# One engine for both copies of a turned query block, row squares on ACT, and a step's scores at its head: three edits to the attention loop of a fused kernel

## The chip, the core and the metric

The program runs on one core of a Trainium2 chip. The metric is the device time of one execution in microseconds, the median over several runs. Engines are named as the profile names them: PE (matmuls and transposes; PEld is its weight load), DVE (VectorE), ACT (ScalarE), POOL (GpSimd) and SP (which here only issues DMAs). The stages and rows below come from one profiled execution; its time stands beside its span in the table.

## What is computed

Three stages in a row, all in float32:

```python
# 1. attention in a sliding window of 64, q k v: (4, 8, 576, 64)
scores = q @ k.T / 8, masked to 0 <= i - j < 64;  attn = softmax(scores);  x = attn @ v
x = x.transpose(0, 2, 1, 3).reshape(2304, 512)
# 2. mixture of 8 experts, one expert per token
xn = x / (norm(x, axis=-1) + 1e-6)
logits = xn @ normalized(expert_emb).T / tau        # tau = 0.1
expert = argmax(logits);  gate = softmax(logits)[expert]
x = gate * (relu(x @ w1[expert]) @ w2[expert])
# 3. dense layer over all 2304 tokens, 512 -> 2048 -> 512
out = (s * relu(x @ w_in) ** 2 + b) @ w_out
```

## The kernel before

**Stages.** The attention loop takes some 157 us, the end of the routing (which token goes to which expert) some 25 us more, and the experts and the dense layer the rest. This change touches the attention loop alone.

**The attention loop.** The work is cut into 36 steps. A step `n` holds two slots, each a tile of 128 tokens (`t`, 0 to 17) and a pair of heads (`hp`, 0 to 3). PE's order and SP's order are written out by hand (`manual_schedule`); DVE, ACT and POOL are ordered by a planner that runs on its own estimate of a timeline, and each engine then works through its list strictly in order. A step of the loop does this for PE, in this order:

- `prepare(n)`: the next 2 or 3 *pieces*. A piece is one head of `k` or `q` of one unit (a batch and a pair of heads; four pieces to a unit, in the order k0, k1, q0, q1): three transposes into one of three PSUM tiles `tp` (L224), and then two copies of 64x288 to `kT` or `qT` (L229 on ACT, L231 on DVE). The two copies write every other column of the same 64 rows. After a unit's last piece, the loads of the unit after next are issued from SP (`load_qk`, L159), and its `v` loads (L185).
- `flips(n)`: four transposes (L268) of the exponentials `pe` of step `n-2` (from step 31 on, of the step one back), into the one PSUM tile `pt`, which ACT copies to `pT` (L270).
- `run(n, HALF)`: what earlier steps left in a list for this step, kinds `TURN` and `WHOLE`: transposes of finished rows of `x` (L375, copied by ACT at L377), matmuls that count and list tokens (L316), the write of `x` (L677, on SP), the first expert's weight loads (L96, on SP).
- `scores(n)`: 16 matmuls (L241) into one of two halves of `spb`; DVE adds the mask and finds the extremum (L249, four times: `sm`, `mn`); in steps 2 to 30 POOL subtracts it (L252); ACT takes the exponential in `exps` (L259, or four times L262 where POOL did not subtract). In step 4 `router_setup` follows, with its loads on ACT's DMA queue.
- `run(n)`: the list's other kinds, `HALF` (the router's logits, L316) and `BEHIND`.
- `fins(n)`: 16 matmuls (L280) with `v` into the one PSUM tile `po`, for step `n-3`; DVE takes the reciprocal of the sum and scales into `xs` (L283, L284, L289).

**Squares of x.** When the last head pair of a tile is done, the sum of squares of its rows (`ss`) is needed, for the norm in `route_norm` (POOL, L460), then `route_gate` (DVE, L467 and on). For tiles 0 to 10 POOL makes it in `squares`: a product (L394) and nine halving additions (L398) for each pair of tiles. For tiles 11 and 12 DVE makes it in one instruction (L381), for 13 to 15 ACT (L384), for 16 and 17 DVE.

Of the kernel before, what the change touches and what calls it, by code (L numbers as in the profile page):

```python
# [8 lines left out]
F32 = mybir.dt.float32  # L9
# [3 lines left out]
AF = mybir.ActivationFunctionType  # L13
ALU = mybir.AluOpType
# [6 lines left out]
def tile_kernel(ctx, tc, q, k, v, emb, tau, w1, w2, w_in, w_out, s_in, b_in, out, x_dram, y_dram, y0_dram, wi_dram, wo_dram):  # L21
    nc = tc.nc
    B, H, S, D = q.shape
    NT, DM = out.shape
# [11 lines left out]
    TF = 13  # L36
    TL = 16
# [42 lines left out]
    x2p = ctx.enter_context(tc.tile_pool(name="x2p", bufs=1))  # L80
# [59 lines left out]
    lp = al.enter_context(tc.tile_pool(name="lp", bufs=1))  # L140
    la = al.enter_context(tc.tile_pool(name="la", bufs=8))
    aw = ac.enter_context(ExitStack())
    at = aw.enter_context(tc.tile_pool(name="at", bufs=1))
# [70 lines left out]
    xs = {}  # L214

    def prep(b, hp):

        kt, qt = qk.pop((b, hp))
        n = (b * NP + hp) % NB
        for nm, src, dst in (("k", kt, kTs[n]), ("q", qt, qTs[n])):  # L220
            for h in range(2):
                pt = ps3.tile([128, QC, QP], F32, tag="tp", name="tp")
                for c in range(QC):
                    nc.tensor.transpose(pt[:, c], src[:, h, c], ident[:QP, :QP])  # L224
                for par in range(2):
                    o = dst[64 * h:64 * h + 64].rearrange("r (c p e) -> r e c p", c=QC, e=2)[:, par]
                    i = pt[64 * par:64 * par + 64]
                    if par == 0 or (nm, h) in TOACT:
                        nc.scalar.activation(o, i, AF.Copy)  # L229
                    else:  # L230
                        nc.vector.tensor_copy(o, i)  # L231
                yield
# [23 lines left out]
    def exps(sm, mn):  # L256
        pe = at3.tile([128, 4, 128], F32, tag="pe", name="pe")
        if mn is None:
            nc.scalar.activation(pe, sm, AF.Exp, scale=-1.0)  # L259
            return pe  # L260
        for j in range(4):
            nc.scalar.activation(pe[:, j], sm[:, j], AF.Exp, bias=mn[:, j:j + 1], scale=-1.0)  # L262
        return pe
# [51 lines left out]
    def add(out, a, b):  # L315
        nc.tensor.matmul(out, a, b, start=False, stop=True, skip_group_check=True)  # L316
# [7 lines left out]
    ss = rp.tile([128, NTT], F32, name="ss")  # L324
# [43 lines left out]
    def rows_of(t):  # L368
        return xs[t][:, t - FIRST[t]]

    def route_turn(t, lp=None):
        xw = rows_of(t)
        tp = ps3.tile([128, ND, 128], F32, tag="tp", name="tpx")
        for c in range(ND):
            nc.tensor.transpose(tp[:, c], xw[:, c * 128:(c + 1) * 128], ident)  # L375
        xt = (lp or at3).tile([128, ND, 128], F32, tag=f"xt{t}" if lp else "xt", name="xt")
        marks.append(nc.scalar.activation(xt, tp, AF.Copy))  # L377
        if t >= LATE:
            sq = (lp or at).tile([128, DM], F32, tag="sq", name="sq")
            if t < TF or t >= TL:  # L380
                nc.vector.tensor_tensor_reduce(out=sq, in0=xw, in1=xw, scale=1.0, scalar=0.0,  # L381
                                               op0=ALU.mult, op1=ALU.add, accum_out=ss[:, t:t + 1])
            else:
                nc.scalar.activation(sq, xw, AF.Square, accum_out=ss[:, t:t + 1])  # L384
        return xt

    def route_logits(t, xt):
        for c in range(ND):
            for o in range(0, 128, 64):
                add(lg[o:o + 64, t], xt[:, c, o:o + 64], enT[:, c])  # L390

    def squares(t, n):
        sq = x2p.tile([128, 1024], F32, tag="xh", name="sq").rearrange("p (s d) -> p s d", s=2)[:, :n]
        nc.gpsimd.tensor_tensor(sq, xs[t], xs[t], op=ALU.mult)  # L394
        c = DM // 2
        while c >= 1:
            o = ss[:, t:t + n].unsqueeze(2) if c == 1 else sq[:, :, :c]
            nc.gpsimd.tensor_tensor(o, sq[:, :, :c], sq[:, :, c:2 * c], op=ALU.add)  # L398
            c //= 2

    def block(kk, ln, a):

# [19 lines left out]
    def route_count(t0, t1):  # L422
        ts_ = slice(t0, t1)
        add(R[:, ts_].rearrange("p t e -> p (t e)"), tri, oh[:, ts_].rearrange("p t e -> p (t e)"))
        for t in range(t0, t1):
            add(R[:, t + 1:], ones, oh[:, t].unsqueeze(1).to_broadcast([128, NTT - t, E]))
# [28 lines left out]
    def listed(t0, t1, j0, j1, Qv):  # L455
        for t in range(t0, t1):
            add(ls[:, j0:j1], lane[:, t], Qv[:, t - t0])
# [208 lines left out]
    def fin(slots, pT):  # L666
        pv(slots, pT)
        t = slots[0][0]
        if slots[-1][1] < NP - 1:
            return  # L670
        ts_ = sorted({t for t, _ in slots})
        nt = len(ts_)
        if t < LATE:
            squares(t, nt)

        def write():
            nc.sync.dma_start(x_dram[t * 128:(t + nt) * 128].rearrange("(s p) n -> p s n", p=128), xs[t])  # L677

        n = now[0]
        if n < len(steps):  # L680
            later(n + 1, write)
        else:
            write()
        if t == TL:
            return
        xts = {}

        def turned(t):
            xts[t] = route_turn(t)

        for j, k_ in enumerate(ts_):
            m = n + (0 if t >= LATE else j)
            later(m + 1, lambda k_=k_: turned(k_), TURN)
            later(m + 2, lambda k_=k_: route_logits(k_, xts[k_]), HALF)
        if ts_[-1] not in ROUTED:
            return
        (t0, t1), d = ROUTED[ts_[-1]]
        q = []
        later(n + d[0], lambda: route_rank(t0, t1), BEHIND)
        later(n + d[1], lambda: route_count(t0, t1))  # L700
        if t1 == TF:
            later(n + d[1], first_weights)
        later(n + d[2], lambda: route_list(t0, t1))
        later(n + d[3], lambda: q.append(part(t0, t1, 0, 2)))
        later(n + d[4], lambda: listed(t0, t1, 0, 2, q[0]))
        if t1 == TL:
            return
        later(n + d[5], lambda: route_norm(t0, t1))
        later(n + d[6], lambda: route_gate(t0, t1), BEHIND)
        later(n + d[7], lambda: q.append(part(t0, t1, 2, 5)), BEHIND)  # L710
        later(n + d[8], lambda: listed(t0, t1, 2, 5, q[1]))
        if t1 == TF:
            later(n + d[9], first_turn)
            later(n + d[4], first_rows)
# [64 lines left out]
            yield  # L779

    now = [0]
    TOACT = (("k", 0), ("k", 1))

    ROUTED = {3: ((0, 4), (4, 5, 6, 7, 9, 10, 11, 12, 14)),
# [3 lines left out]
    LATE = 11  # L788
# [6 lines left out]
    TURN, WHOLE, HALF, BEHIND = range(4)  # L795

    def later(n, do, kind=WHOLE):
        todo.setdefault(n, []).append((kind, do))

    def run(n, end=9):  # L800

        q = todo.get(n, [])
        for kind in range(end):
            for k_, do in [x for x in q if x[0] == kind]:
                q.remove((k_, do))
                do()
        if not q:
            todo.pop(n, None)
# [13 lines left out]
    need = [4 * (max(u for us in used[:n + 1] for u in us) + 1) for n in range(len(steps))]  # L822
# [32 lines left out]
    def flips(n):  # L855
        while len(pts) < len(steps) and len(pts) + lag(len(pts)) <= n:
            pts.append(flip(pes[len(pts)]))
# [16 lines left out]
    done = [0]  # L874
    pes, pts = [], []

    def prepare(n):
        want = max(need[m] + (AHEAD if m > n else 0) - RATE * (m - n) for m in range(n, len(steps)))
        while done[0] < min(want if n else need[0] + 2, 4 * len(units)) and free(done[0] // 4, n):
            next(pieces)  # L880
            done[0] += 1
        assert done[0] >= need[n]

    with tc.manual_schedule(engines={mybir.EngineType.PE, mybir.EngineType.SP}):
        for n, s in enumerate(steps):
            now[0] = n
            prepare(n)
            t = s[0][0]
            if t not in xs:
                nt = 1 if t == s[1][0] else 2  # L890
                xs[t] = (lp if t == TL else xp).tile([128, nt, DM], F32, tag=f"xs{nt}", name="xs",
                                                            **({} if t == TL else {"bufs": 2 * nt}))
                xs[s[1][0]] = xs[t]
            flips(n)
            run(n, HALF)
            sm, mn = scores(n, s)
            if n == 4:
                router_setup()
            pes.append(exps(sm, mn))
            run(n)  # L900
            fins(n)
            values()
        N = len(steps)
        for n in range(N, N + 2):
            now[0] = n
            flips(n)
            some(n - N)
            fins(n)
            if n in todo:
                run(n)  # L910
# [395 lines left out]
```

## Time and profile before

| | |
|---|---|
| median of 3 runs | 847.34 us (847.22 to 849.98) |
| the profiled execution | 851.04 us, of which its span is 849.2 us |
| PE busy | 790.2 us (93% of the span), mean granted clock 0.961 |
| DVE busy | 516.7 us (61%) |
| ACT busy | 387.1 us (46%) |
| POOL busy | 237.2 us (28%) |

Busy shares are means over stages with different limits: behind the attention and routing PE hardly rests, inside the attention loop it does. The granted clock is PE's: 1.0 is 2.4 GHz, 0.5 is 1.2 GHz, and a mean between them is a share of time at either.

### The profile page before, as it was taken

How to read it: one execution, taken by the hardware profiler on the slowest of the kernel's cores; microseconds unless marked ns; L12 is line 12 of the kernel's file. 1: busy time of each engine (PE TensorE's matmuls, PEld its weight loads, DVE VectorE, ACT ScalarE, POOL GpSimd, SP SyncE). 2: the span in 40 equal slices, each digit the busy share in tenths (PEclk: the TensorE clock that was granted, in tenths of full speed). 3: DMA queues.
4: the chain of work that ended last, by engine and by line, in shares of the span. 5: the costliest groups of instructions: out<-in, count | busy, mean ns of one | idle time of the engine just before them, and what ended most of it. 6: DMA issues, size and time to landing. Idle time of an engine off the chain costs nothing. (4 is left out here: it accounts for less than half of the span.)

```text
span 849.2 us, 16607 instructions
## 1 busy us (share of the span) xinstructions
PE 790.2 (93%) x6350; PEld 724.4 (85%) x6350; DVE 516.7 (61%) x1310; ACT 387.1 (46%) x770; POOL 237.2 (28%) x248
## 2 busy tenths in 40 slices
PE   7887887878999999989899999999999999999996
PEld 5676765778999999979899999999999999999885
DVE  4566586675687787689665555566665444444442
ACT  6686656413435355364364444444445333323331
POOL 3374775241202433434302222122210110101110
PEclk9997897878999999999999999999999999999998
DMA  9865925215749787769265322234323111100000
GB/s 204 191 177 159 218 65 195 88 30 202 244 130 297 238 275 243 271 217 311 99 220 180 100 100 100 79 121 125 124 88 101 61 40 50 50 25 25 26 26 25
DMA packets 100642, 117.16 MB, mean 138 GB/s; under 512 B 38884, under 2 KB 72164, under 8 KB 100560
## 3 DMA queue, kind: packets, MB, share of 16 engines
q1 hardware_dynamic: 91072, 99.11, 38.7%
q0 software_dynamic: 3232, 10.24, 3.5%
q10 hardware_dynamic: 6256, 6.72, 2.4%
q8 instruction: 51, 0.84, 0.4%
q14 instruction: 31, 0.25, 0.1%
HBM read 91.52 MB, written 24.53 MB: 137 GB/s over the span
## 5 line engine op out<-in xcount | busy, mean ns | idle before, releaser
L126 PE MATMUL p<-xl,wh 128*128 128x256 f32 x576 | 162.4, 282 | 0.0
L126 PE MATMUL p<-xh,wh 128*128 128x256 f32 x576 | 162.2, 282 | 0.0
L126 PE MATMUL p<-xh,wl 128*128 128x256 f32 x576 | 161.7, 281 | 0.0
L1213 ACT ACTIVATE r<-p 128x256 f32<-128x256 f32 x144 | 55.2, 384 | 167.9 <-PE p L126 163.6
L1214 DVE SCALAR_TENSOR_TENSOR r<-r,s_bc 128x256 f32<-128x256 f32 x144 | 79.9, 558 | 78.0 <-ACT r L1213 77.6
L1037 POOL TENSOR_TENSOR fl<-fl,fs 128x512 f32<-128x512 f32 x32 | 45.9, 1436 | 251.7 <-DVE fs L1036 219.3
L126 PE MATMUL p<-wh,gh 128*128 128x512 f32 x288 | 113.0, 392 | 0.0
L126 PE MATMUL p<-wl,gh 128*128 128x512 f32 x288 | 113.0, 392 | 0.0
L126 PE MATMUL p<-wh,gl 128*128 128x512 f32 x288 | 113.0, 392 | 0.0
L126 PEld LDWEIGHTS p<-xh,wh 128*128 128x128 f32 x576 | 108.8, 189 | 0.7
L126 PEld LDWEIGHTS p<-xl,wh 128*128 128x128 f32 x576 | 108.6, 189 | 0.8
L126 PEld LDWEIGHTS p<-xh,wl 128*128 128x128 f32 x576 | 109.0, 189 | 0.0
L88 DVE TENSOR_TENSOR wl<-raw,wh 128x1024 fp32r<-128x1024 f32 x72 | 102.8, 1433 | 6.0 <-ACT wh L87 5.7
L87 ACT ACTIVATE wh<-raw 128x1024 fp32r<-128x1024 f32 x80 | 83.4, 1057 | 6.4 <-DMA raw<-wo_dram 2.3
L126 PE MATMUL p<-hh,wh 128*128 128x256 f32 (+5 forms) x256 | 78.7, 307 | 0.0
L126 PE MATMUL p<-hl,wh 128*128 128x256 f32 (+5 forms) x256 | 76.9, 301 | 0.0
L126 PE MATMUL p<-hh,wl 128*128 128x256 f32 (+5 forms) x256 | 76.9, 300 | 0.0
L1220 ACT ACTIVATE gh<-r,b_bc 128x256 fp32r<-128x256 f32 x144 | 72.5, 503 | 7.2 <-DVE r L1214 6.9
L1252 POOL DMA_INDIRECT out_dram<-o,ids x18 | 18.8, 1047 | 203.8 <-DVE o L1251 182.4
L1221 DVE SCALAR_TENSOR_TENSOR gl<-r,b_bc,gh 128x256 fp32r<-128x256 f32 x144 | 71.2, 495 | 3.1 <-ACT gh L1220 3.1
L132 PE MATMUL tp<-xh,wh 128*128 128x256 f32 (+6 forms) x288 | 55.9, 319 | 12.2 <-DVE hl L749 5.5
L126 PEld LDWEIGHTS p<-wh,gl 128*128 128x128 f32 x288 | 54.1, 188 | 12.2
(225 smaller groups left out, 1522.2 us busy)
## 6 DMA issues: line engine op xcount, KB each, us to landing
raw<-in_moe_w_dram SPq DMA_DIRECT2D x64, 512.0 KB, 4.9
raw<-y_dram SPq DMA_DIRECT2D x18, 512.0 KB, 3.8
vb<-in_v_dram SPq DMA_DIRECT2D x64, 128.0 KB, 3.8
fr<-in_moe_w_in_dram SPq DMA_DIRECT2D x16, 512.0 KB, 5.3
fr<-in_moe_w_out_dram SPq DMA_DIRECT2D x16, 512.0 KB, 4.1
k<-in_k_dram SPq DMA_DIRECT2D x32, 144.0 KB, 3.5
q<-in_q_dram SPq DMA_DIRECT2D x32, 144.0 KB, 3.4
x_dram<-xs SPq DMA_DIRECT2D x8, 512.0 KB, 3.1
```

Of the source, the lines that this page charges most:

```text
L87: a = nc.scalar.activation(hi, src, AF.Copy)
L88: return a.ins, le.tensor_tensor(lo, src, hi.bitcast(F32), op=ALU.subtract).ins
L126: nc.tensor.matmul(ps, a[x], b[y], start=first and j == 0, stop=last and j == 2)
L132: nc.tensor.matmul(ps, x, y, start=j == 0, stop=j == len(k) - 1)
L1037: nc.gpsimd.tensor_tensor(lf, lf, sg.bitcast(F32), op=ALU.mult)
L1213: nc.scalar.activation(r, ps, AF.Relu)
L1214: nc.vector.scalar_tensor_tensor(r, r, s_bc, r, op0=ALU.mult, op1=ALU.mult)
L1220: nc.scalar.activation(gh, r, AF.Identity, bias=b_bc)
L1221: nc.vector.scalar_tensor_tensor(gl, r, b_bc, gh.bitcast(F32), op0=ALU.add, op1=ALU.subtract)
L1252: nc.gpsimd.indirect_dma_start(out=out, out_offset=bass.IndirectOffsetOnAxis(ap=ids[:, k:k + 1], axis=0), in_=o, in_offset=None)
```

## The change

Three edits.

1. In `prep`, the copies of piece q0 go both to ACT and those of q1 both to DVE. Before, each of the two pieces had its first copy on ACT and its second on DVE. The number of copies on either engine stays as it is: per unit six on ACT and two on DVE.
2. `squares` is gone; in `route_turn` ACT makes the sum of squares for every tile up to 15 (one `Square` with an accumulator each). That takes the work of tiles 0 to 10 from POOL and that of 11 and 12 from DVE.
3. A step of the loop begins with `scores(n)` and `exps`, unless a piece that they need is still missing; then come `prepare(n)`, `flips(n)` and the whole of `run(n)`. By the loop's own arithmetic no piece is missing in steps 1 to 35.

```diff
@@ prep
-                    if par == 0 or (nm, h) in TOACT:
+                    if (nm, h) in TOACT:
                         nc.scalar.activation(o, i, AF.Copy)
                     else:
                         nc.vector.tensor_copy(o, i)
@@ route_turn
-        if t >= LATE:
-            sq = (lp or at).tile([128, DM], F32, tag="sq", name="sq")
-            if t < TF or t >= TL:
-                nc.vector.tensor_tensor_reduce(out=sq, in0=xw, in1=xw, scale=1.0, scalar=0.0,
-                                               op0=ALU.mult, op1=ALU.add, accum_out=ss[:, t:t + 1])
-            else:
-                nc.scalar.activation(sq, xw, AF.Square, accum_out=ss[:, t:t + 1])
+        sq = (lp or at).tile([128, DM], F32, tag="sq", name="sq")
+        if t >= TL:
+            nc.vector.tensor_tensor_reduce(out=sq, in0=xw, in1=xw, scale=1.0, scalar=0.0,
+                                           op0=ALU.mult, op1=ALU.add, accum_out=ss[:, t:t + 1])
+        else:
+            nc.scalar.activation(sq, xw, AF.Square, accum_out=ss[:, t:t + 1])
@@ squares, and its call in fin
-    def squares(t, n):
-        sq = x2p.tile([128, 1024], F32, tag="xh", name="sq").rearrange("p (s d) -> p s d", s=2)[:, :n]
-        nc.gpsimd.tensor_tensor(sq, xs[t], xs[t], op=ALU.mult)
-        c = DM // 2
-        while c >= 1:
-            o = ss[:, t:t + n].unsqueeze(2) if c == 1 else sq[:, :, :c]
-            nc.gpsimd.tensor_tensor(o, sq[:, :, :c], sq[:, :, c:2 * c], op=ALU.add)
-            c //= 2
...
-        if t < LATE:
-            squares(t, nt)
...
-    TOACT = (("k", 0), ("k", 1))
+    TOACT = (("k", 0), ("k", 1), ("q", 0))
@@ the loop over steps
-            prepare(n)
+            if done[0] < need[n]:
+                prepare(n)
...
-            flips(n)
-            run(n, HALF)
             sm, mn = scores(n, s)
             if n == 4:
                 router_setup()
             pes.append(exps(sm, mn))
+            prepare(n)
+            flips(n)
             run(n)
             fins(n)
```

## Rows read from the trace of the kernel before

**Rows 1.** Stages: length, busy of PE, PEld, DVE, ACT, POOL; granted clock; DMA.

```profile
21.26:42.77 21.51, 17.72 (x263) 13.57 (x262) 12.61 (x74) 14.88 (x32) 7.83 (x11) 0.92 0.84 191
42.77:57.88 15.11, 13.39 (x248) 11.10 (x248) 9.28 (x54) 12.09 (x26) 13.86 (x24) 1.00 0.80 213
76.24:98.94 22.70, 20.10 (x321) 16.70 (x320) 12.47 (x67) 16.72 (x37) 17.43 (x26) 0.88 0.79 193
116.88:130.54 13.66, 10.92 (x195) 9.37 (x194) 11.10 (x51) 6.63 (x13) 10.35 (x14) 0.88 0.21 79
130.54:157.28 26.74, 21.65 (x282) 17.45 (x279) 17.85 (x97) 16.91 (x39) 11.48 (x6) 0.70 0.59 204
175.78:849.20 673.42, 653.61 (x4392) 613.30 (x4391) 399.33 (x727) 277.24 (x539) 141.86 (x105) 0.98 0.41 133
```

**Rows 2.** Waits of PE from 0 to 200 us: total, times, longest.

```profile
PE tp L224 <- DMA k<-in_k_dram: 2.0, 1, 2.0
PE spb L241 <- DVE mn L249: 1.4, 4, 0.5
```

**Rows 3.** Timeline of ACT around 24 us: start, length, idle before and its releaser.

```profile
22.42 0.43 ACT L229 ACTIVATE qT<-tp 64x288 f32<-64x288 f32 x1
...
25.53 0.63 ACT L259 ACTIVATE pe<-sm 128x512 f32<-128x512 f32 x1 [2.21 <-POOL sm L252]
26.19 0.41 ACT L229 ACTIVATE qT<-tp 64x288 f32<-64x288 f32 x1
```

**Rows 4.** Timeline of DVE in the same stretch.

```profile
22.89 0.46 DVE L231 COPY qT<-tp 64x288 f32<-64x288 f32 x1 [1.59 <-ACT qT L229]
23.38 0.29 DVE L249 CUSTOM_DVE_ANT_0 sm<-spb,mask 128x128 f32<-128x128 f32 x1
...
26.63 0.46 DVE L231 COPY qT<-tp 64x288 f32<-64x288 f32 x1 [1.42 <-ACT qT L229]
```

**Rows 5.** Timeline of POOL in the same stretch.

```profile
24.46 1.04 POOL L252 TENSOR_TENSOR sm<-sm,mn 128x512 f32<-128x512 f32 x1 [2.72 <-DVE mn L249]
```

**Rows 6.** Groups by line and shape, 0 to 160 us: busy, mean ns, idle before.

```profile
L259 ACT ACTIVATE pe<-sm 128x512 f32<-128x512 f32 x29 | 18.2, 628 | 16.1 <-POOL sm L252 15.9
...
L231 DVE COPY qT<-tp 64x288 f32<-64x288 f32 x32 | 14.7, 461 | 22.5 <-ACT qT L229 22.1
...
L381 DVE CUSTOM_DVE_ANT_0 sq<-xs 128x512 f32<-128x512 f32 x2 | 2.2, 1076 | 0.1
```

**Rows 7.** Groups of ACT by line and shape, the whole span.

```profile
L384 ACT ACTIVATE sq<-xs 128x512 f32<-128x512 f32 x3 | 1.9, 627 | 0.1
L166 ACT ACT_TABLE_LOAD x1 | 1.3, 1283 | 1.7 <-PEq L1286 1.7
L384 ACT ACTIVATION_READ_ACCUMULATOR sq<-xs 128x1 f32 x3 | 0.6, 192 | 0.0
```

**Rows 8.** Groups of POOL by line, 40 to 130 us.

```profile
L398 POOL TENSOR_TENSOR sq<-sq 128x256 f32<-128x256 f32 (+8 forms) x48 | 22.6, 470 | 2.9
L394 POOL TENSOR_TENSOR sq<-xs 128x1024 f32<-128x1024 f32 (+1 forms) x6 | 10.5, 1750 | 0.7 <-DVE val L481 0.4
```

**Rows 9.** Timeline of DVE, 116 to 135 us.

```profile
116.47 2.37 DVE L451 TENSOR_TENSOR Qv<-Q,val 128x480 bf16<-128x480 bf16 x1
...
127.24 1.00 DVE L467 TENSOR_SCALAR nrm<-nrm 128x4 f32<-128x4 f32 x1 [1.65 <-POOL nrm L460]
...
134.56 0.55 DVE L451 TENSOR_TENSOR Qv<-Q,val 128x384 bf16<-128x384 bf16 x1
```

**Rows 10.** Timeline of PE, 121 to 151 us.

```profile
121.54 0.67 PE L241 MATMUL spb<-kT,qT 64*64 64x128 f32 x16
...
129.93 0.55 PE L375 MATMUL tpx<-ident,xs 128*128 128x128 f32 x3 [2.74 <-DVE xs L289]
...
135.80 1.13 PE L241 MATMUL spb<-kT,qT 64*64 64x128 f32 x16
...
150.06 1.21 PE L268 MATMUL pt<-ident,pe 128*128 128x128 f32 x4 [3.12 <-ACT pe L262]
```

## The prediction, made before the changed kernel ran

> **What bounds the kernel now.** I read the table of stages first. From 175.78 us to the end PE is busy 653.6 of 673.4 us [rows 1]; nothing that the change touches lies there, so what the attention loop gains or loses moves the end by as much, and the question is what the loop's 157 us wait for. The starts of the scores cut it into stages, and there PE is busy 17.72 of 21.51, 13.39 of 15.11, 20.10 of 22.70, 10.92 of 13.66 and 21.65 of 26.74 us [rows 1].
>
> Part of the busy time is itself loss. The 16 score matmuls of a step take 0.67 us at 121.54 and 1.13 at 135.80, behind a wait of 2.74 us [rows 10]: the granted clock fell from 2.4 to 1.2 GHz, and the slow work wastes 0.41 of its time. A mean clock of 0.92 over 21.51 us is 16% at the low level, 3.4 us, of which 1.4 are lost; 0.88 over 13.66 us loses 1.3; 0.70 over 26.74 us loses 6.6 (each an upper estimate, as if PE were busy in all of the slow time).
>
> Then I laid the timelines of ACT, DVE and POOL over each other around 24 us, because in the waits and groups two sums stand out: DVE idles 22.1 us for ACT's `qT` copy, and ACT idles 15.9 us for POOL's `sm` [rows 6]. They are one ring. ACT copies the first half of a query piece (22.42, 0.43 us); DVE, which has waited 1.59 us for that, copies the second (22.89, 0.46) and only then gets to the scores (23.38, four of them to 24.3); POOL, idle 2.72 us, subtracts (24.46, 1.04); ACT, idle 2.21, takes the exponential (25.53, 0.63), and its next query copy stands behind it (26.19) [rows 3, 4, 5]. One turn is 26.63 - 22.89 = 3.74 us [rows 4], against a mean of 21.51 / 6 = 3.59 per step in this stage, and against PE's own work of (17.72 - 1.4) / 6 = 2.7 [rows 1]. The ring, not an engine's work, sets the pace. What closes it is that the two halves, on two engines, are kept in order though they write different columns.
>
> Later the limit is another. From 116.88 to 130.54 DVE is busy 11.10 of 13.66 us [rows 1] with routing work stretched by POOL: one `Qv` of 480 columns takes 2.37 us at 116.47, where one of 384 takes 0.55 at 134.56, and L467 waits 1.65 us for POOL's norm and takes 1.00 itself [rows 9]. Behind it in DVE's order stands the `xs` for which PE waits 2.74 us at 129.93 [rows 10].
>
> **The change part by part.** The profiled execution takes 851.04 us, its span 849.2; the median of the runs is 847.34. I make the sum against the execution and carry the difference to the median.
>
> *Copies.* Counts on both engines are unchanged; a piece that one engine empties costs 0.43 + 0.43 on ACT or 0.46 + 0.46 on DVE [rows 3, 4], and the wait of DVE for ACT, 22.1 us [rows 6], has nothing left to cause it. Where does that stall go? In the stage from 21.26 to 42.77 PE stands idle 3.79 us and loses 1.4 to the clock: at most 5.2 us. Next in line is ACT, busy 14.88 us, which is less than PE's 16.3. I take 60%, 3.2 us, since ACT's copy of `pt` still sits between copies and exponentials. Ends: nothing (the planner puts another wait into the ring's place) and 5.2.
>
> *Squares off POOL.* Gone are 22.6 + 10.5 = 33 us of POOL [rows 8] and two squares of 1.08 on DVE [rows 6]; added are 13 on ACT, each 0.627 + 0.192 = 0.82 us [rows 7], 10.7 us. Between 116.88 and 130.54 DVE loses the two squares (2.15), the stretch of `Qv` (2.37 against 0.55 x 480 / 384 = 0.69: 1.7), the wait of 1.65 and 0.8 of L467 [rows 6, 9]: 6.3 us of its 13.66. What is late next is PE, 10.92 - 1.3 = 9.6 us, and ACT, 6.63 + 4 x 0.82 = 9.9 [rows 1, 7]. So at most 13.66 - 9.9 = 3.8; I take 2.7, as the norm still has to go from ACT through POOL to DVE. Ends: 0 and 3.8.
>
> *Squares onto ACT.* The cover is ACT's idle time. In the stage from 42.77 to 57.88 ACT is busy 12.09 us; four squares make 15.4 in a stage of 15.11 [rows 1, 7]: full. From 76.24 to 98.94 it is 16.72 + 5 x 0.82 = 20.8 of 22.70, and there PE waits 2.0 us for a `k` load anyway [rows 1, 2]. I charge 0.5 us; without cover the nine squares cost 7.4.
>
> Here a rule of the Trainium skill speaks against the edit. ACT's table was loaded once, in 1.28 us, in the whole span, though three `Square` lie between exponentials [rows 7]; so the new ones load nothing either. The Trainium skill (ScalarE: Activation LUTs, Table sets: the hidden batching unit) says that functions of different sets cost a table load at every switch, and does not name the square in its list for the exponential's set. By its 2.7 us, 13 squares with a switch to and fro would cost an estimated 70 us; the trace excludes that.
>
> *Scores first.* No work is added or dropped; with the scores go 16 matmuls, four DVE instructions, one on POOL and one to four exponentials, moved ahead of the pieces, the flip and the list. Scores issue no DMA, so SP's order of loads and writes stays; only in step 4 do `router_setup`'s two ACT-queue loads and its transposes now come ahead of that step's pieces. PE at the head of a step now waits for `mn` of two steps before, with pieces and flip queued behind; that wait is 1.4 us in four today [rows 2] and its distance stays two steps. The gain is where a wait stood in front of ready scores: at 150.06 PE waits 3.12 us for an exponential, with scores behind it that then take the slow 1.13 [rows 10]. They fit into the wait: 1.1 us. Ends: 0 and 1.1.
>
> *Clock.* From 130.54 to 157.28 the low level costs up to 6.6 us. The slow stretch begins right behind the wait of 2.74 us [rows 10] that the second edit shortens, so I count 2.0; the stage's own wait of 3.12 remains, and with it a later fall. Ends: 0 and 6.6.
>
> Sum: -3.2 - 2.7 + 0.5 - 1.1 - 2.0 = -8.5 us. The profiled execution would take 842.5, the median 847.34 - 8.5 = **838.8 us**. With every bound at its best the gains are 5.2 + 3.8 + 1.1 + 6.6 = 16.7, so 830.6; with none, and 0.5 to 1.5 paid for the squares, 848 to 849.
>
> **Rivals.**
>
> *The planner rebuilds a wait* (0.20). ACT still runs in a planned order; if an exponential stands ahead of the copies as before, ACT idles for POOL and `pt` comes late, and DVE's order may again put routing ahead of `xs`. For it: ACT's 15.9 us of waiting for `sm` [rows 6] come from a list made on estimated times. Against: nothing then holds DVE, so `sm` starts earlier. The first term goes to 0, the second and the clock to half: -1.4 - 1.1 - 1.0 + 0.5 = -3.0, **844.3 us**, no measurable change.
>
> *The scores wait for their own pieces* (0.12). Before, 2 or 3 pieces came between a unit's last query piece and its scores; now, in steps 2, 4, 6, 8 and 10, one. DVE needs 0.92 us for q1 and may be busy with `sm` for 0.9; PE has one piece, a flip and `po` in between, some 1.5 us. With all of 0.9 exposed in five steps, 4.5 us come back: -4.0, **843.3 us**. Against: DVE is free of its stalls, so I expect 0.1 in each.
>
> *ACT becomes the bound* (0.12), the slower side. ACT takes its list in order. A square waits for `xs`, behind PE's `po` and DVE; planned too early, it holds up the `pT` copy that PE's next flip needs. Each of 13 would cost its 0.82 and a wait such as those for `sm` today, 15.9 / 29 = 0.55 for each exponential [rows 6]: 17.8 us against gains of 9.0, so **856.1 us**. It decides from 1.0 us exposed per square (13.2 us) for a kernel slower by 4.2. For it: the full stage from 42.77; against: ACT is busy 6.63 of 13.66 and 16.91 of 26.74 us in the others [rows 1].
>
> **How the numbers follow.** My forecast has 0.56, its own range 831 to 842.5; the three rivals 0.20, 0.12 and 0.12. Half a percent, 4.2 us, is about what a measurement of this kernel tells from none: faster means under 843.1, slower over 851.6. Faster: the forecast nearly whole (0.53), a third of each of the first two rivals (0.11); slower: 0.10 of the last; the rest is the same. The range from 831.5 to 848.5 leaves out the last rival and half of a tenth at the fast end.
>
> **What would show it.** Right: no idle time of DVE before L231 for ACT; starts of scores some 3.0 us apart between 21 and 43 us; no 2 us `Qv`; L467 without its wait; PE's wait for `xs` near 130 under 1.5 us and the clock up behind it; the last scores ahead of the flip that waits. Wrong: ACT busy nine tenths or more with PE waiting for L270, L229 or L377; PE waiting for `qT` in front of L241; or the stage behind 157 us longer by what the loop gained, as its wait for routing is set by DVE and POOL.

## The result, and the profile after

The changed kernel takes **836.12 us** (median of 4 runs, 834.43 to 840.44) against 848.13 (847.22 to 849.98) for the kernel before, timed in turn on one chip: a ratio of 0.9863 with a 95% interval of [0.9819, 0.9908], a gain of some 12 us where 8.5 were forecast. The total was right. Most of its terms were not: the edit priced lowest among the gains brings most of it (by the ratios below 9.7 us alone and 6.9 as the last of the three), and one that was to bring 2.7 us brings nothing that can be measured beside the other two.

| | before | after |
|---|---|---|
| the profiled execution, its span | 851.04, 849.2 us | 840.44, 838.7 us |
| PE busy, mean granted clock | 790.2 us, 0.961 | 788.7 us, 0.964 |
| DVE, ACT, POOL busy | 516.7, 387.1, 237.2 us | 507.8, 393.9, 203.5 us |

The profiled execution is the longest of the four; the granted clock of the other three was 0.972 to 0.976. Below L380 the new kernel's line numbers are lower: the square on ACT is L383, `Qv` L441, POOL's and DVE's `nrm` L450 and L457, the routing's `oh` and `pr` L410 and L499.

First the stages, cut at starts of scores as in [rows 1] (same columns). The first row and the last three answer to that group's first row and last three, from the scores of the same steps on; the fifth ends, as there, with the loop's last flip. The second begins as that group's second does, with step 10; the cuts at 48.91 and 64.88 are the starts of scores nearest to where the clock falls and where it is back.

```profile
22.06:38.31 16.25, 15.74 (x261) 12.21 (x258) 13.01 (x74) 14.17 (x30) 6.58 (x10) 1.00 1.02 215
38.31:48.91 10.60, 8.27 (x116) 6.40 (x112) 5.70 (x27) 10.08 (x24) 3.69 (x5) 0.93 1.16 261
48.91:64.88 15.97, 15.97 (x183) 13.68 (x181) 8.14 (x49) 7.80 (x18) 3.12 (x3) 0.51 0.27 80
116.19:125.51 9.32, 9.26 (x193) 7.88 (x189) 5.51 (x38) 7.51 (x19) 4.24 (x5) 1.00 0.32 117
125.51:150.92 25.41, 20.90 (x296) 17.38 (x293) 17.30 (x104) 18.32 (x43) 12.42 (x7) 0.73 0.62 215
168.77:838.70 669.93, 651.85 (x4392) 611.46 (x4391) 397.63 (x727) 277.21 (x539) 141.51 (x105) 0.99 0.41 134
```

Two stages that waited now hardly do. The first fell from 21.51 to 16.25 us, 2.71 a step, with PE busy for 15.74 of them; the one before the loop's last part from 13.66 to 9.32, PE busy for 9.26. One stage is new, and bad: from 48.91 to 64.88 PE is busy all the time at a granted clock of 0.51. The last row begins where the wait for `oh` ends; from there on 4392 matmuls run in both kernels and the change has no work. So of the 10.5 us between the two spans 6.9 are the loop's and the routing's (175.70 us fell to 168.77), and 3.5 lie in a part that the edits don't touch, at a clock of 0.99 for 0.98.

The ring's signature is gone from the groups by line and shape, 0 to 160 us (of before in [rows 6]):

```profile
L259 ACT ACTIVATE pe<-sm 128x512 f32<-128x512 f32 x29 | 18.2, 627 | 7.9 <-POOL sm L252 7.9
L231 DVE COPY qT<-tp 64x288 f32<-64x288 f32 x32 | 14.6, 457 | 2.2 <-PE tp L224 1.5
L383 ACT ACTIVATE sq<-xs 128x512 f32<-128x512 f32 x16 | 10.1, 628 | 1.5 <-DVE xs L289 1.2 <-DVE oh L410 0.2
L383 ACT ACTIVATION_READ_ACCUMULATOR sq<-xs 128x1 f32 x16 | 3.1, 191 | 0.0
```

DVE's 22.1 us of waiting for ACT before L231 are now 1.5 us for PE's transposes. ACT's 15.9 us for `sm` halved, but that sum over the loop is no sign of the ring: with the copies alone it is 16.8 us and with copies and order 17.5, where DVE's wait for ACT is gone as well. Only 5.2 of the 15.9 us lie in the first stage, and these are 0.2 in the changed kernel. DVE's timeline shows the pair of copies as one entry of two, with no wait before it:

```profile
26.38 0.28 DVE L249 CUSTOM_DVE_ANT_0 sm<-spb,mask 128x128 f32<-128x128 f32 x1
27.34 0.93 DVE L231 COPY qT<-tp 64x288 f32<-64x288 f32 x2
29.34 0.28 DVE L249 CUSTOM_DVE_ANT_0 sm<-spb,mask 128x128 f32<-128x128 f32 x1
```

What PE waits for, 0 to 200 us (total, times, longest):

```profile
PE rt L316 <- DVE oh L410: 7.6, 1, 7.6
PE po L280 <- DVE xs L289: 5.1, 3, 2.3
...
PE tpx L375 <- ACT kT L229: 2.9, 4, 1.4
...
PE spb L241 <- DVE qT L231: 2.0, 1, 2.0
...
PE spb L241 <- DVE mn L249: 1.0, 1, 1.0
```

The wait for `oh` that ends the routing is 7.6 to 8.0 us long in each of the fourteen kernels of this study, wherever the loop before it ends.

### The profile page after: what moved, and what is told of

It reads as the page before. It is cut to its first block, busy times and chain, and to the rows that moved or that the text cites. A ratio compares the mean times of both kernels' runs of the same rounds, so it can differ in the third digit from the quotient of the medians.

```text
span 838.7 us, 16564 instructions
## 1 busy us (share of the span) xinstructions
PE 788.7 (94%) x6350; PEld 722.9 (86%) x6350; DVE 507.8 (61%) x1306; ACT 393.9 (47%) x796; POOL 203.5 (24%) x188
## 4 chain that ended last, share of the span: by engine, by line
PE 50%; issue 0%; DMA 0%; POOLq 0%; DVE 0%
PE p L126 49%; PE tp L132 1%; DMA out_dram<-o,ids 0%; POOLq L1290 0%; DVE o L1240 0%; POOLq L1241 0%
## 5 line engine op out<-in xcount | busy, mean ns | idle before, releaser
L126 PEld LDWEIGHTS p<-wh,gh 128*128 128x128 f32 x288 | 54.1, 188 | 11.4
```

Source lines behind the costliest of these rows:

```text
L126: nc.tensor.matmul(ps, a[x], b[y], start=first and j == 0, stop=last and j == 2)
```

## The experiments

The twelve kernels were timed in three groups of four, each group in turn with the kernel before on one chip, with 6 or 12 runs of each kernel; the median of the kernel before is 849.14, 847.97 and 849.70 us in the three. Ratios stand with their 95% intervals; they are taken from the single runs and differ from the quotients of these medians by up to 0.2%. A quotient of two ratios is uncertain by 0.4 to 0.6%, worked out as if the two were independent. Each kernel has one profile, so a stage in it is one sample. How far two samples can lie apart shows where two kernels issue the same instructions in the same order on PE, DVE, ACT and POOL: the order alone and its early half do so from step 4 to step 25, in 75.17 and 78.74 us.

### Each edit alone

**The copies alone**: in `prep`, the first edit and nothing else.

```diff
-                    if par == 0 or (nm, h) in TOACT:
+                    if (nm, h) in TOACT:
-    TOACT = (("k", 0), ("k", 1))
+    TOACT = (("k", 0), ("k", 1), ("q", 0))
```

> Only the copies are paired. Ring theory: the ring between ACT's and DVE's halves of a query piece is broken by this edit alone, so DVE's wait for ACT before its qT copies falls from 22.1 us to under 3, scores starts between steps 4 and 10 come 3.0 us apart instead of 3.59, and the kernel gains some 3 us (844 to 846). Rival, the order does it: with scores still behind pieces and flip the planner keeps ACT waiting for POOL's subtraction, DVE's wait goes but steps stay at 3.5 us and the time at 848.

848.26 us against 849.14: 0.9978 [0.9949, 1.0007]. In the trace (windows, columns as in [rows 1]) the first stage gains its 3.0 us, and the stretch from the scores of step 25 to those of step 35 loses as much (first this stretch in the kernel before, then two rows of the kernel with the copies alone):

```profile
106.31:152.32 46.01, 34.36 (x523) 27.48 (x522) 35.83 (x182) 28.36 (x60) 28.49 (x28) 0.84 0.44 146
...
21.73:40.21 18.48, 16.03 (x263) 12.33 (x262) 12.93 (x74) 15.03 (x32) 7.20 (x11) 1.00 1.04 211
...
105.98:155.01 49.03, 36.02 (x523) 28.32 (x522) 33.61 (x181) 28.30 (x60) 25.85 (x24) 0.80 0.44 143
```

No wait of DVE for ACT is left before L231. So the ring was there and the edit opens it. In this execution what it saves is lost again later; whether that holds for the median the interval doesn't tell, since it has room for the whole 3.0 us, and the profiled execution (852.47 us) is 4.2 us above the median.

**The squares alone**: `squares` and its call removed, `Square` on ACT for every tile up to 15, as in the diff above.

> Only the squares go to ACT. Theory of the prediction: DVE is freed between 116 and 130 us (no Qv of 2.4 us, L467 without its wait), PE's wait of 2.7 us at 130 falls under 1.5 and the slow clock behind it shortens: 4 to 5 us gained there, 0.5 lost to ACT's fuller queue, so 844. Rival, seen in the changed kernel's trace: ACT is full between 38 and 47 us, PE waits for a kT copy and drops to the low clock for 16 us, which costs some 6.5 us and eats the gain: 847 to 850.

853.67 us against 849.14: 1.0063 [1.0034, 1.0091], slower. The stage of 13.66 us behind step 28 does shorten, to 12.04, and the ring stays closed (3.59 us a step, DVE's wait for ACT 25.3 us); the stretch from step 25 to 35 takes 48.54. Neither expectation reached so high a time.

**The order alone**: the third edit.

```diff
             now[0] = n
-            prepare(n)
+            if done[0] < need[n]:
+                prepare(n)
...
-            flips(n)
-            run(n, HALF)
             sm, mn = scores(n, s)
...
             pes.append(exps(sm, mn))
+            prepare(n)
+            flips(n)
             run(n)
```

> Only the order changes. Theory of the prediction: the order is worth 1 us at the end of the loop, the ring stays (DVE's wait for ACT about 22 us), so 847. Rival, the order is the main edit: scores a step further ahead of their flip give the ring slack, steps 4 to 10 come 3.1 us apart, and 840 or less is reached by this alone.

840.04 us against 849.14: 0.9886 [0.9840, 0.9932]. An edit priced at 1.1 us brings 9.7. Its windows, the first stage and the stretch from step 25 to 35:

```profile
22.98:39.13 16.15, 15.54 (x262) 12.18 (x258) 12.30 (x73) 14.06 (x30) 5.34 (x8) 1.00 0.89 201
...
98.15:136.08 37.93, 29.75 (x527) 23.87 (x524) 31.69 (x181) 23.20 (x49) 24.00 (x27) 0.96 0.42 136
```

The first stage is as short as in the whole change, 2.69 us a step, though the two halves of a piece are still split; and the late stretch is 8.1 us shorter, its clock at 0.96 instead of 0.84. DVE still waits for ACT, by the list of one line's waits:

```profile
  ACT qT L229: 12.9, 15
```

but 12.9 us instead of 22.1, and in the first stage PE, busy 15.54 of 16.15 us, hardly waits with it: the scores' four DVE instructions now come ahead of the copy that waits, as in its timeline (the last of the four, then the copy):

```profile
30.28 0.28 DVE L249 CUSTOM_DVE_ANT_0 sm<-spb,mask 128x128 f32<-128x128 f32 x1
...
31.50 0.46 DVE L231 COPY qT<-tp 64x288 f32<-64x288 f32 x1 [0.93 <-ACT qT L229]
```

So the ring can be opened at either of two places.

### Each edit left out

**Without the copies** (edits 2 and 3):

> Squares on ACT and the order, copies split as before. If the order has already given the ring its slack, the paired copies add nothing and this is as the change: 836 to 839. If the ring still binds, DVE's wait for ACT before qT is over 13 us and this is slower than the change by 3 us or more: 839 to 844.

841.84 us against 847.97: 0.9948 [0.9925, 0.9971]. DVE still waits 15.9 us for ACT before L231.

**Without the squares** (edits 1 and 3):

> Paired copies and the order, squares left on POOL and DVE. If squares on ACT cost more than they free, as alone (5 us slower), this is faster than the whole change: 831 to 835, with the clock up between 48 and 64 us. If in the new order they free DVE late in the loop without harm, it is slower than the change: 838 to 841.

836.48 us: 0.9875 [0.9844, 0.9906], the same as the whole change. The stage behind step 28 takes 9.40 us here, against 9.32 with the squares moved, and the `Qv` of 480 columns, 2.37 us in [rows 9], takes this long with POOL still making the squares (its product comes 0.9 us behind, at 114.77):

```profile
L451 DVE TENSOR_TENSOR Qv<-Q,val 128x480 bf16<-128x480 bf16 x1 | 0.7, 658 | 0.0
```

But the collision of the two isn't what makes the stage long. With the copies alone, in the old order, this `Qv` is as short, and the stage takes 14.22 us:

```profile
115.31 0.66 DVE L451 TENSOR_TENSOR Qv<-Q,val 128x480 bf16<-128x480 bf16 x1
...
128.29 1.00 DVE L467 TENSOR_SCALAR nrm<-nrm 128x4 f32<-128x4 f32 x1 [2.32 <-POOL nrm L460]
```

```profile
131.25 0.90 PE L375 MATMUL tpx<-ident,xs 128*128 128x128 f32 x3 [3.67 <-DVE xs L289]
```

In the old order DVE's `nrm`, for which it waits 0.5 to 2.3 us, stands in this stage ahead of the `xs` that PE waits for, and PE's wait is 1.65 to 3.67 us (the kernel before, the copies, the squares, both). With the order alone, and with order and copies, `nrm` comes behind the stage (at 121.43 and 125.91 us, the stages ending at 118.56 and 122.58), and no wait of PE for `xs` in it is above 0.41 us; with squares and order, and with all three edits, it stands behind the stage's last `xs`, and PE has no such wait. That is what goes with the shorter stage; it was not changed by itself.

**Without the order** (edits 1 and 2):

> Paired copies and squares on ACT in the old order. If the first two edits only add up (0.2% faster, 0.6% slower), 849 to 853; if the order is what makes them useful, no faster than that. If, as the prediction had it, they carry two thirds of the gain, 840 to 843.

845.05 us against 849.70: 0.9944 [0.9920, 0.9968], between the two ranges expected.

With the single edits these give what each edit is worth in each company:

| edit | with neither other | with the first other | with the second other | with both |
|---|---|---|---|---|
| copies (others: squares, order) | 0.9978 | 0.9882 | 0.9989 | 0.9915 |
| squares (others: copies, order) | 1.0063 | 0.9966 | 1.0063 | 0.9988 |
| order (others: copies, squares) | 0.9886 | 0.9897 | 0.9886 | 0.9919 |

The order gives about 1% wherever it is added. The squares cost 0.6% while the copies are split and nothing that can be measured once they are paired; the copies are worth little by themselves and about 1% beside the squares on ACT.

The profiles of the same eight kernels say where. Lengths in us, from the scores of one step to those of another; the last column is a part of the one before it:

| kernel | steps 4 to 10 | 10 to 25 | 25 to 35 | 28 to 31 |
|---|---|---|---|---|
| before | 21.51 | 63.54 | 46.01 | 13.66 |
| copies | 18.48 | 65.77 | 49.03 | 14.22 |
| squares | 21.52 | 66.25 | 48.54 | 12.04 |
| copies, squares | 18.20 | 63.91 | 44.05 | 11.45 |
| order | 16.15 | 59.02 | 37.93 | 11.38 |
| order, copies | 15.88 | 66.11 | 37.64 | 9.40 |
| order, squares | 16.17 | 59.87 | 40.24 | 9.48 |
| all three | 16.25 | 68.39 | 39.52 | 9.32 |

In every company the order shortens the first stretch, by 2.0 to 5.4 us, and the third, by 4.5 to 11.4. The middle one varies by up to 9 us in another pattern; the two long ones beside the order belong to executions 4 us above their kernels' medians.

**Squares on ACT only from tile 9 on** (the whole change, but POOL keeps tiles 0 to 8).

```diff
-        sq = (lp or at).tile([128, DM], F32, tag="sq", name="sq")
-        if t >= TL:
...
+        if t >= 9:
+            sq = (lp or at).tile([128, DM], F32, tag="sq", name="sq")
+            if t >= TL:
...
+        if t < 9:
+            squares(t, nt)
```

> The whole change, but the squares of tiles 0 to 8 stay on POOL; only 9 to 12 move to ACT. If the squares of the early tiles cost more on ACT than they free (PE's wait for kT and 16 us of slow clock from 48 us on in the changed kernel), this keeps the clock up between 48 and 64 us, saves up to 6 us and beats the change: 830 to 833. If the slow stretch has another cause, or POOL's squares hold up the subtraction again, it is no better than the change: 836 to 840.

836.88 us against 849.14: 0.9861 [0.9824, 0.9898]. It bears on the bad stage. In the changed kernel the clock falls behind the wait of 1.44 us that PE's timeline shows at 46.57 (and three waits of 0.38 us or less before it), and the scores then take 1.13 us:

```profile
46.57 0.66 PE L375 MATMUL tpx<-ident,xs 128*128 128x128 f32 x4 [1.44 <-ACT kT L229]
47.15 0.87 PE L316 MATMUL rt<-enT,xt 128*64 128x8 f32 x16
48.91 1.13 PE L241 MATMUL spb<-kT,qT 64*64 64x128 f32 x16
```

ACT is busy for 10.08 of the 10.60 us up to 48.91; its timeline has the copy of `k` that PE waits for behind the last of four squares:

```profile
45.05 0.63 ACT L383 ACTIVATE sq<-xs 128x512 f32<-128x512 f32 x1
...
45.68 0.83 ACT L229 ACTIVATE kT<-tp 64x288 f32<-64x288 f32 x2
```

With these squares on POOL the steps 10 to 13 keep their full clock:

```profile
38.16:49.58 11.42, 10.81 (x194) 8.95 (x190) 6.12 (x36) 8.68 (x19) 10.13 (x15) 1.00 1.08 262
```

and from the scores of step 10 to those of step 14 this kernel takes 15.1 us instead of 22.8. Yet the median is no better: in this kernel too PE waits, in other places (2.19 us for `mn` at 58.42), and the clock from 53.27 to 63.50 is 0.73. Removing one slow stretch shows in its place and not in the total.

Nor do ACT's squares always bring the slow stretch. In the three other kernels that have them all on ACT the steps 10 to 14 take 16.19 us (squares alone), 15.07 (with the copies) and 15.78 (with the order), at a clock of 1.00. The last of these has nearly the same wait at the same matmul, and its next scores take 0.67 us:

```profile
46.62 0.66 PE L375 MATMUL tpx<-ident,xs 128*128 128x128 f32 x4 [1.42 <-DVE qT L231]
...
48.29 0.67 PE L241 MATMUL spb<-kT,qT 64*64 64x128 f32 x16
```

### Which part of the order

**Scores ahead of the flips and the list, behind the pieces.**

```diff
             prepare(n)
...
-            flips(n)
-            run(n, HALF)
             sm, mn = scores(n, s)
...
             pes.append(exps(sm, mn))
+            flips(n)
             run(n)
```

> Of the order alone, only half: pieces first as before, then scores, then flip and list. If the gain of the order (some 9 us alone) comes from the longer way from a step's scores to their flip, so that DVE, POOL and ACT are done when PE gets there, this half has most of it: 840 to 843. If it comes from PE having scores to do while pieces wait for their copies, it has little: 846 to 850.

862.31 us against 847.97: 1.0174 [1.0140, 1.0208], 14 us slower, where neither expectation had it above 850. The first stage and steps 25 to 35:

```profile
23.40:48.76 25.36, 20.86 (x259) 15.55 (x258) 12.64 (x73) 13.67 (x29) 5.88 (x9) 0.91 0.63 154
...
118.44:161.53 43.09, 33.32 (x515) 27.44 (x515) 30.48 (x179) 24.97 (x53) 24.14 (x24) 0.80 0.38 123
```

Here the ring is tighter: 4.23 us a step, DVE's wait for ACT 30.1 us. In DVE's timeline:

```profile
37.99 0.46 DVE L231 COPY qT<-tp 64x288 f32<-64x288 f32 x1 [1.58 <-ACT qT L229]
42.97 0.46 DVE L231 COPY qT<-tp 64x288 f32<-64x288 f32 x1 [2.81 <-ACT qT L229]
```

The late stretch gains 2.9 us all the same.

**Scores ahead of the pieces, behind the flips and the list's first half.**

```diff
-            prepare(n)
+            if done[0] < need[n]:
+                prepare(n)
...
             sm, mn = scores(n, s)
...
             pes.append(exps(sm, mn))
+            prepare(n)
             run(n)
```

> The other half of the order alone: flip and list first, then scores, then pieces. If the way from scores to flip makes the gain, this has little of it, 846 to 850; if the pieces behind which the scores stood make it, most: 840 to 843.

850.36 us: 1.0026 [0.9999, 1.0053]. The mirror image: the first stage opens (2.86 us a step, 17.18 us in all), the late stretch takes 6.5 us more than before:

```profile
23.68:40.86 17.18, 16.14 (x263) 12.43 (x262) 12.81 (x74) 14.98 (x32) 6.89 (x10) 1.00 0.86 198
...
103.63:156.18 52.55, 36.42 (x533) 28.76 (x532) 33.55 (x186) 28.52 (x61) 26.17 (x24) 0.81 0.47 141
```

**Scores ahead of the flips, with paired copies** (the 14 us slower kernel and the first edit).

> The half order that ran 14 us slower than before (pieces, scores, flip, list), with the paired copies added. If that half order is slow because it closes the ring between ACT and DVE more tightly (turns of 4.0 us against 3.74), pairing the copies opens it: steps 4 to 10 at 3.0 us or less instead of 4.2, 7 us and more gained there, 845 to 855 in all. If something else makes it slow, it stays above 858.

848.66 us against 849.70: 0.9976 [0.9950, 1.0003]. Against 1.0174 the pairing alone is worth 1.9%, and the first stage falls to 2.82 us a step:

```profile
21.28:38.21 16.93, 15.88 (x258) 12.04 (x257) 13.15 (x74) 14.43 (x30) 6.38 (x10) 1.00 0.95 199
```

That is the ring shown from both sides: where it is tightest, opening it is worth most. Against the kernel before, though, its first stage is 4.6 us shorter and its median 1.0 (by the interval at most 4.2): from step 10 to 25 it takes 68.86 us instead of 63.54.

**The new order in steps 0 to 26 only, and from step 27 on only** (two kernels; `head = n >= 27` in the other).

```diff
             now[0] = n
-            prepare(n)
+            head = n < 27
+            if not head or done[0] < need[n]:
+                prepare(n)
...
-            flips(n)
-            run(n, HALF)
+            if not head:
+                flips(n)
+                run(n, HALF)
...
             pes.append(exps(sm, mn))
+            if head:
+                prepare(n)
+                flips(n)
             run(n)
```

> The new order in steps 0 to 26 alone (where there are pieces), the old one from 27 on. If the order's gain is the ring's, which only pieces make, it has most of the order's 9 us: 840 to 843. If the gain is made in the steps without pieces, it has little: 845 to 848.

> The new order from step 27 on alone. If the gain is the ring's: no better than before, 847 to 850. If scores ahead of flip and list keep PE from waiting for xs and for exponentials in the last ten steps, 4 us or more: 841 to 845.

Early: 847.16 us against 849.70, 0.9981 [0.9957, 1.0005]. Late: 845.81, 0.9960 [0.9941, 0.9979], between the two expectations. Together they make 0.6%, where the whole order makes 1.1%; the quotient of the two, 0.9945, is uncertain by 0.55%, so that the halves fall short of the whole is at the edge of what these runs can tell. The early one has the first stage at 2.69 us a step and then, from step 25 to 35, back in the old order:

```profile
102.14:154.33 52.19, 37.77 (x539) 30.36 (x535) 34.45 (x187) 28.68 (x61) 27.24 (x27) 0.75 0.43 136
```

Up to step 26 this kernel has the full order's program, from there the old one. Against 37.93 us with the new order throughout, this stretch is 14.3 us longer: 8.0 of it are PE's busy time (37.77 against 29.75, at a clock of 0.75 against 0.96), 6.2 its idle time. Two of PE's waits in it, by the timeline:

```profile
126.53 0.90 PE L375 MATMUL tpx<-ident,xs 128*128 128x128 f32 x3 [2.80 <-DVE xs L289]
140.47 1.35 PE L268 MATMUL pt<-ident,pe 128*128 128x128 f32 x4 [3.80 <-ACT pe L262]
```

The kernel with the order alone waits here 0.54 us for `xs` and not at all for `pe` (its longest waits in the stretch are 1.67 us for `mn` and 1.64 for `pT`):

```profile
120.47 0.55 PE L375 MATMUL tpx<-ident,xs 128*128 128x128 f32 x3 [0.54 <-DVE xs L289]
```

The early kernel's profiled execution was its longest (854.04 us), so 14.3 is at the upper end; by the medians the late half, added to the early one, is worth 0.9886 / 0.9981 = 0.9905, some 8 us, with an uncertainty of 0.52%. Added to the old order it is worth 3.4.

## Why the prediction came out as it did

**The diagnosis of the ring was right.** Paired copies remove DVE's wait for ACT (22.1 us to none), and the kernels with the scores ahead of the flips show that this wait sets the pace: 4.23 us a step with split copies, 2.82 with paired. The forecast of about 3.0 us a step is what the copies alone give (3.08).

**Copies, -3.2: right as a price for the stage, doubtful as one for the end.** Alone, the stage gave 3.0 us and the execution 1.9 (interval: a gain of 4.3 to a loss of 0.6), so this kernel can't decide; beside the order the copies give 0.9 us or so, within the noise. The step that failed stands at the head of the prediction: "what the attention loop gains or loses moves the end by as much" holds for the loop as a whole, but I used it for one stage of the loop. With the scores ahead of the pieces alone the first stage gained 4.3 us and the median at most 0.1 by its interval; with the early half of the order it gained 5.4 and the median at most 3.7. These two took 52.55 and 52.19 us from step 25 to 35 instead of 46.01, the copies alone 49.03. But the kernel with copies and squares, in the old order as well, gained 3.3 us early and took 44.05: the old order doesn't always take the gain back.

**Scores first, -1.1, held to be a bound from both sides: this is the term that failed.** It measured 1.0% in the mean of four comparisons, 7 to 10 us. I looked for places "where a wait stood in front of ready scores", found one of 3.12 us and priced it alone. Two things were missed. First, the order also acts on the ring, since PE's order sets when DVE gets its scores: with the scores ahead of the pieces their `sm` reaches DVE before the copy that waits, and the first stage falls to 16.15 us with the copies still split. So the gain of the first stage, booked under copies, comes with the order too, and only once: 3.0 us with the copies alone, 5.4 with the order, 5.6 with both. Second, the waits late in the loop are waits for what the scores set going: scores issued at a step's head make `sm`, `pe` and in the end `xs` come sooner, and the waits of 2.80 and 3.80 us that the old order leaves there are 0.54 and none with the order. In the changed kernel the predicted sign was met:

```profile
146.22 0.72 PE L241 MATMUL spb<-kT,qT 64*64 64x128 f32 x16
...
150.56 0.33 PE L268 MATMUL pt<-ident,pe 128*128 128x128 f32 x1 [0.28 <-ACT pe L262]
```

The wait in front of the flip, 3.12 us in [rows 10], is 0.28, and the last scores, now ahead of it, take 0.72 us instead of 1.13: not scores fitted into a wait, but a wait that has gone.

**Squares off POOL, -2.7: failed in attribution.** The stage it was priced on gained 4.3 us, above the bound of 3.8, but gains as much with copies and order and the squares on POOL (9.40 us). The reading that failed is that `Qv`'s 2.37 us and the squares make the stage long: with the copies alone that `Qv` takes 0.66 us and the stage 14.22. What the kernels with a stage of 9.3 to 11.4 us and the new order have in common is that PE no longer waits for an `xs` behind DVE's wait for the norm, and the order does that too, so most of the relief was counted for the wrong edit. In the old order the squares are worth 1.6 us in that stage, or 2.8 with paired copies. The sign "no 2 us `Qv`" came true without meaning what it was to mean; L457's wait for the norm did not go:

```profile
124.00 0.17 DVE L457 TENSOR_SCALAR nrm<-nrm 128x4 f32<-128x4 f32 x1 [0.91 <-POOL nrm L450]
...
133.06 0.56 DVE L441 TENSOR_TENSOR Qv<-Q,val 128x384 bf16<-128x384 bf16 x1
```

**Squares onto ACT, +0.5.** The place was right: the stage behind 42.77 us was called full, and there, in steps 10 to 14, the `kT` that PE waits 1.44 us for stands behind ACT's squares. That this wait cost PE its clock is not shown, since a wait of 1.42 us in the same place, in the kernel without the copies, did not. The sign of the rival in which ACT becomes the bound (ACT above nine tenths, PE waiting for L229) is met in this one stage, 10.08 of 10.60 us. It did not decide: moving those squares back changes nothing that can be measured. Both terms of the squares together are 0.9988 in the full change, some 1 us with an uncertainty of 4 to 5, where -2.2 us were forecast; while the copies are split they cost 0.6%, about 5 us. There the added ACT work lies in an ACT list that DVE waits for (25.3 us before L231 for 22.1), which fits, but I have not shown that the 5 us come from there: in the one profile of the squares alone 2.7 us more lie between steps 10 and 25 and 2.5 between 25 and 35. The price of one square was right (0.628 and 0.191 us). The Trainium skill (ScalarE: Activation LUTs, Table sets: the hidden batching unit) would have a table loaded at each change to a function of another set. The square is no such change: with 16 squares among the exponentials the whole span of the changed kernel still has one load, as the prediction read from three:

```profile
L166 ACT ACT_TABLE_LOAD x1 | 1.3, 1283 | 1.7 <-PEq L1275 1.7
```

**Clock, -2.0: nothing in the profiled execution.** The wait for `xs` fell as predicted, 2.74 us to 0.67, and the clock held behind it, until the next wait:

```profile
127.54 0.55 PE L375 MATMUL tpx<-ident,xs 128*128 128x128 f32 x3 [0.67 <-DVE xs L289]
...
133.77 1.03 PE L316 MATMUL rt<-enT,xt 128*64 128x8 f32 x16 [1.47 <-DVE pr L499]
135.69 1.13 PE L241 MATMUL spb<-kT,qT 64*64 64x128 f32 x16
```

The window from 125.51 is at 0.73 where that of before is at 0.70, and a new slow stretch stands at 48.91. Between 8 us and the end of the wait for `oh`, PE is busy 133.19 us at a clock of 0.86 (before: 132.91 at 0.87); all 6.9 us gained there are idle time. With the order alone it is 125.62 us at 0.93, and in the kernel that keeps tiles 0 to 8 on POOL 125.52 at 0.92: in these PE is busy 7 us less. Which execution gets the clock is not settled by an edit alone: the same program from step 4 to 25 ran at 0.95 with the order alone and at 0.89 with its early half, and the other three executions of the changed kernel were 3 to 6 us shorter than the profiled one at a mean clock of 0.972 to 0.976. What the term is worth in the median stays open.

**The rivals.** A planner's wait in the ring's place was not seen: the early stage ran at PE's pace. Scores waiting for their own pieces: one wait of 2.0 us for `qT`, against 4.5 priced.

**The total** came out near by luck, because errors partly cancelled. Added in the turn order, copies, squares, the ratios put 9.7, 0.9 and 1.0 us to the three; in the turn copies, squares, order 1.9, 2.9 and 6.9. Forecast were 1.1 for the order, 3.2 for the copies and 4.2 for the squares with the clock: 5.8 to 8.6 us too little for the first, 2.6 to 5.5 too much for the others.

**What stays open.** Why an early gain is given back in some kernels and not in others: in the profiles of the three that lost it there the stretch of steps 25 to 35 has more idle time of PE (13.0 to 16.1 us for 11.7) and a lower clock (0.75 to 0.81 for 0.84), but what is late in it first was not isolated. Whether the halves of the order make less than the whole: the medians leave it at the edge of their uncertainty, and the profiles that agree with it are one execution each. And what brings the clock down at 48.91.

## What to carry to other kernels

When two halves of one small job sit on two engines that must finish in order, look for a ring: a step's length that no engine's work explains, and two long waits that point at each other, both counted in that stage and not over the whole loop. It can be opened by giving the job to one engine or by issuing first what the ring delays; price the two together, because the gain comes only once. Price a change of order not only by the waits that it fills but by the waits later on for what it starts sooner, and time edits in each other's company: the same one cost 0.6% and nothing here. Ask a second kernel whether a slow instruction sets a stage's length before pricing its removal. After this change the longest single wait up to 200 us is PE's 7.6 us for `oh`, which none of the edits shortened.

## What the runs showed of the chip that was not expected

A short wait can be followed by far more than its length, and need not be. Behind the wait of 1.44 us at 46.57 the granted clock is 0.51 for 15.97 us from 48.91 on, the level of 1.2 GHz, although PE is busy through all of them; the kernel that keeps those squares on POOL has neither the wait nor the slow stretch, and from the scores of step 10 to those of step 14 it takes 15.1 us instead of 22.8. But a wait of 1.42 us at the same matmul, without the paired copies, left the clock at 1.00 for the next 6.68 us, and one of 1.67 us for `mn` at 111.78, with the order alone, was followed by scores of 0.67 us. Ahead of the fall PE stood idle 2.33 of the 10.60 us from 38.31 to 48.91; ahead of the wait that did no harm, 1.61 of the 9.10 us from 39.19 to 48.29. What decides between them was not tried.

The time of one and the same kernel goes with the clock it is granted: 23 runs of the unchanged kernel beside the first four experiments reach from 841.84 us at a mean clock of 0.977 to 852.75 at 0.958, a spread as large as what was to be measured. Not every pair of them keeps that order.
